# q and k of batches 4 to 7 by GpSimd casts and transfer transposes, global sums and v's copies moved to the period's head

## The chip, the cores and the metric

The kernel runs on one core of one Trainium2 chip. The time is that of one execution on the device, in microseconds (us); before the change it is 334.76 us, the median of 14 runs (332.55 to 339.53). All row times below count from the start of the profiled execution's span.

## What is computed

Two layers in one kernel, for 8 batches of 576 rows: an attention with a window and global rows, then an MLP mixer (over rows, then over channels). Cut to what matters:

```
q, k, v: [8, 8, 576, 64] float32         # batch, head, row, dim
mask = |i - j| <= 32, or i is one of 8 global rows, or j is one
attn = softmax(where(mask, q k^T / 8, -1e9))
x = (attn v), heads side by side         # [8, 576, 512]
h = relu(x^T w_tok1) w_tok2              # over rows: 576 -> 256 -> 576
u = x + h^T
out = u + relu(u w_ch1) w_ch2            # over channels: 512 -> 1536 -> 512
```

Only the window and the global rows and columns are computed; the rest of the scores is never formed.

## The kernel before

**Stages.** Per batch b, all in float16 with float32 sums. `load_qk` and `load_rest` (lines 114 to 120) bring q and k in float32 by SP's DMA queue into `lq`, `lk` (512 rows, four consecutive rows per partition) and `lqr`, `lkr` (the last 64 rows); there is one such buffer of each. `cast_qk` (380) makes float16 copies `qn`, `kn` (two buffers each), for one head pair or, with p None, the last rows. `T` (396) transposes one head pair of q and of k by eight TensorE matmuls with the identity into PSUM, and `TE` (417) copies the result in row order into `qTs`, `kTs` (one DVE copy each, lines 406 and 412). `TR` (421) does the last 64 rows, `globals_` (391) puts the eight global queries into `qTs`. `S_` (443) computes a head pair's windowed scores (22 small matmuls in two parts), `SX` (466) takes the exponential on ScalarE into `e_all`, and `SM` (472) multiplies by the masks on DVE (`eg` at line 476, `e_all` twice at 481). `GK` (508) makes the scores of the global rows, with an exponential into `lf` and a mask product (532). `load_v16` (358) loads v straight to float16 by GpSimd's DMA queue, five transfers, into `vsh`; `v_odd` (371) makes `vod`, a copy of v moved by 64 partitions, by two DVE copies of 64x2112 (373, 374). `OG` (534) sums v over the global rows (20 matmuls) and spreads the result over blocks into `rf` on DVE (544). `PV` (647) makes one 128-row tile of the attention from `lf` x `rf` and `e_all` x `vsh`/`vod`, and normalizes it on DVE (678, 679). `M1` and `M2` (684, 708) are the mixer over rows, with the sum u on DVE (721, 724); `M3` (726) transposes u by DMA transposes on SP's queue. `M4` and `M4l` (749, 760) are the first channel matmul with relu on ScalarE, `M5` (774) the second, in halves of six matmuls of 128x512, with the last sum on DVE (785, 788) into `osb`, which SP writes out. Batches share the last 64 rows in pairs, so `M4l` and a fifth `M5` tile stand in odd periods only.

**Order.** Every engine runs its own instructions in the order in which they are written; the program is written as a weave. "Period b" is the loop's pass b (line 1037): its dense units are `dense(b)` (M4, M4l, M5 of batch b), and between them stand units of the batches behind: in the first half those of n = b + 1 (PV, M1, M2, M3) and the casts and transposes of m = b + 2, in the second half scores and masks of m. `play` (822) walks a list written out by hand, in which each `D` stands for the next dense unit. Period 0 has its own list (`period_0`, 835), and period 1 is woven by cost (`merge` with `sparse2`, 796). Periods 2 to 7 use `first_half` (852) and `second_half` (880); the first half holds the first 12 dense units (15 in odd periods), the second the rest, those left over coming last. "Head b" is the start of the first half of period b.

Before the change the head has M4, M4, then PV; OG and the masks come at the end of the second half before it, and v_odd between the third and the fourth scores. The ten casts of m stand between the units of the first half on ScalarE; three of the four transposes stand late in the first half, the fourth in the second half.

**Buffers.** PSUM is handed out in turn by three pools: `pss` (two buffers of two banks), `psv` (one of two banks) and `psm` (two of one bank). M4 and M5 use `psm`; each tile there waits until the one two before it has been read out. Scores use `pss`; OG, GK, even PV tiles and odd-numbered T use `psv` in most batches.

Of the kernel before, what the change touches and what calls it, by code (L numbers as in the profile page):

```python
# [9 lines left out]
F16 = mybir.dt.float16  # L10
# [5 lines left out]
P = 128  # L16
NT = 5
NG = 8
WIN = 32
GW = 2 * NG  # L20
QS = P + NG
HQ = 64
# [22 lines left out]
def kernel(  # L45
# [12 lines left out]
    nc = tc.nc  # L58
# [312 lines left out]
    def v_odd(b, hs=slice(0, H), eng=nc.vector):  # L371
        i = b % 2
        eng.tensor_copy(out=vod[i][HQ:P, :, hs], in_=vsh[i][HQ:P, 0 : NT - 1, hs])  # L373
        eng.tensor_copy(out=vod[i][0:HQ, :, hs], in_=vsh[i][0:HQ, 1:NT, hs])  # L374

    def castv(p):
        hs = slice(2 * p, 2 * p + 2)
        nc.gpsimd.tensor_copy(out=vsh[0][:, :, hs, 0:D], in_=lv[:, :, hs])
# [9 lines left out]
    def casts(b):  # L388
        return [lambda ti=ti, p=p: cast_qk(b, ti, p, nc.scalar.copy) for p in (None, 0, 1, 2, 3) for ti in range(2)]
# [27 lines left out]
    def TE(b, p):  # L417
        TEq(b, p)
        TEk(b, p)

    def TR(b):
        pr = (psm if b in (0, 2) else psv)([P, 2, 4, NP * 16], name=f"pr_{b}")
        sel = ident.rearrange("p (n r x) -> p r n x", n=NP, r=2)
        for ti, n in enumerate((qr, kr)):
            for i in range(4):
                for par in range(2):
                    nc.tensor.matmul(
                        pr[64 * par : 64 * par + 64, ti, i, :], lhsT=n[b % 2][:, i, :], rhs=sel[:, par], start=True, stop=True
                    )
        st[b]["pr"] = pr  # L430
        if b > 0:
            TRE(b)
# [39 lines left out]
    def SM(b, p):  # L472
        e2 = e_all[:, 2 * p : 2 * p + 2]
        if b > 0:
            gc = bass.AP(tensor=e2.tensor, offset=e2.offset, ap=[e2.ap[0], [QS, NT], [ES, 2], [1, NG]])
            nc.vector.tensor_tensor(
                out=eg[:, :, 2 * p : 2 * p + 2, 0:NG], in0=gc, in1=egm.unsqueeze(2).to_broadcast([P, NT, 2, NG]), op=ALU.mult
            )
        bm = bandm.rearrange("p c x -> p (c x)")[:, 0:ES]
        for par in range(2):  # L480
            nc.vector.tensor_mul(out=e2[:, par], in0=e2[:, par], in1=bm)  # L481
# [26 lines left out]
    def GK(b):  # L508
        s = st[b]
        ps = (psv if b != 2 else pss)([P, 2, 512], name=f"gk_{b}")  # L510
        for p in range(NP):
            o = ps[32 * p : 32 * p + 32]
            qv = qTs[b % 2][:, p, :, NG:QS]
            w = kgz[:, b, p, :]
            nc.tensor.matmul(o[:, 0, 0:384], lhsT=w, rhs=qv[:, 0:3], start=True, stop=True)
            nc.tensor.matmul(o[:, 1, 0:128], lhsT=w, rhs=qv[:, 3], start=True, stop=True)
            nc.tensor.matmul(o[:, 1, 128:192], lhsT=w, rhs=qv[:, 4, 0:LAST], start=True, stop=True)
        s["gk"] = ps
        if b > 0:
            LX(b)  # L520
            LM(b)
# [12 lines left out]
    def OG(b):  # L534
        s = st[b]
        ps = (psv if b != 2 else pss)([P, 2, VW], name=f"og_{b}")
        for c in range(NT):
            for p in range(NP):
                nc.tensor.matmul(
                    ps[32 * p : 32 * p + 32], lhsT=eg[:, c, 2 * p : 2 * p + 2, :],  # L540
                    rhs=vsh[b % 2][:, c, 2 * p : 2 * p + 2, :], start=(c == 0), stop=(c == NT - 1),
                )
        rf = mb.tile([P, NP, 2, VW], F16, tag="rf", name=f"rf_{b}")
        nc.vector.tensor_tensor(
            out=rf, in0=ps.unsqueeze(1).to_broadcast([P, NP, 2, VW]),
            in1=blk.rearrange("p (n r) -> p n r", r=2).unsqueeze(3).to_broadcast([P, NP, 2, VW]), op=ALU.mult,
        )
        s["rf"] = rf
# [243 lines left out]
    def t(b, p):  # L792
        T(b, p)
        TE(b, p)

    def sparse2():
        b, n = 2, 3
        cs = casts(n)

        def cast(k):  # L800
            return [(0.0, c) for c in cs[2 * k : 2 * k + 2]]

        u = [(0.0, lambda: (load_rest(n), load_qk(n, slice(0, H))))]
        u += [(1.0, s2(b, 1)), (0.0, lambda: SM(b, 1)), (1.0, lambda: t(b, 3)), (1.5, s2(b, 2)), (0.0, lambda: SM(b, 2)), (0.0, lambda: v_odd(b))]
        u += [(0.3, lambda: GK(b)), (0.3, lambda: S_(b, 3, 0)), (1.8, lambda: S_(b, 3, 1)), (0.0, lambda: SM(b, 3))]
        u += [(2.5, lambda: OG(b))]
        u += [(2.0, lambda: PV(b, 0)), (2.0, lambda: PV(b, 1)), *cast(0), (2.0, lambda: PV(b, 2)), *cast(1)]
        u += [(0.0, lambda: PV(b, 3)), (1.0, lambda: [M1(b, ch) for ch in range(3)]), *cast(2)]
        u += [(2.0, lambda: PV(b, 4)), *cast(3), (3.0, lambda: [M1(b, ch) for ch in range(3, NT)]), *cast(4)]
        u += [(0.0, lambda: (load_rest(n + 1), load_qk(n + 1, slice(0, H))))]  # L810
        u += [(0.0, lambda: load_v16(n))]
        u += [(1.3, lambda: (M2(b, 0), M3(b, 0))), (1.0, lambda: (M2(b, 1), M3(b, 1)))]
        u += [(2.0, lambda: (M2(b, 2), M3(b, 2) if b % 2 else None))]
        u += [(1.0, lambda: (globals_(n), TR(n)))]
        u += [(1.2, lambda p=p: t(n, p)) for p in range(NP)]
        for p in range(NP):
            u += [(0.3, lambda p=p: S_(n, p, 0)), (2.2, lambda p=p: S_(n, p, 1)), (0.0, lambda p=p: SM(n, p))]
            if p == 2:
                u += [(0.5, lambda: GK(n)), (0.0, lambda: v_odd(n))]
        return u  # L820

    def play(steps, d):
# [9 lines left out]
    def s2(b, p):  # L832
        return lambda: (S_(b, p, 0), S_(b, p, 1))

    def period_0():
        n, m = 1, 2
        D = None
        c2 = casts(m)
        c1 = [lambda ti=ti, p=p: cast_qk(1, ti, p, nc.scalar.copy) for p in (2, 3) for ti in range(2)]
        u = [D, D, D, D, D, D, lambda: TR(n), lambda: globals_(n), D, lambda: t(n, 0), *c1[:2], D]  # L840
        u += [lambda: t(n, 1), *c1[2:], lambda: (load_qk1(2), load_v16(2)), D, s2(n, 0), D, lambda: t(n, 2), lambda: SM(n, 0), D, s2(n, 1), D]
        u += [lambda: t(n, 3), lambda: SM(n, 1), s2(n, 2), lambda: v_odd(n), D, lambda: SM(n, 2), lambda: GK(n), s2(n, 3), D]
        u += [lambda: SM(n, 3), lambda: OG(n), D, lambda: PV(n, 0), lambda: PV(n, 1), D, lambda: PV(n, 2), lambda: PV(n, 3), D]
        u += [*c2, lambda: PV(n, 4), lambda: [M1(n, ch) for ch in range(NT - 1)], D, lambda: M1(n, NT - 1), lambda: globals_(m), D]
        u += [lambda: M2(n, 0), lambda: M2(n, 1), lambda: TR(m), D, lambda: M3p(n, 0), lambda: t(m, 0)]
        u += [lambda: M3p(n, 1), lambda: (M2(n, 2), M3(n, 2)), lambda: t(m, 1)]
        u += [s2(m, 0), lambda: t(m, 2), lambda: SM(m, 0)]
        return u

        return u  # L850

    def first_half(b):
        n, m = b + 1, b + 2
        D = None
        cs = casts(m) if m < B else []

        def c(k):
            return cs[2 * k : 2 * k + 2]

        def tt(p):  # L860
            return [lambda: t(m, p)] if m < B else []

        def pv(tau):
            return lambda: PV(n, tau)

        if n == B:
            return []
        u = [D, *([lambda: OG(n)] if b == 2 else []), D, pv(0), pv(1), *c(0), D, *c(1), D, pv(2), pv(3), *c(2), D, lambda: [M1(n, ch) for ch in range(3)], D]
        if b == 2:
            u += [lambda: gather_t(1)]  # L870
        u += [pv(4), *c(3), D, lambda: M1(n, 3), D, *([lambda: TR(m)] if m < B else []), lambda: M1(n, 4), *c(4)]
        if m < B:
            u += [lambda: load_v16(m), lambda: globals_(m)]
        if m + 1 < B:
            u += [lambda: (load_rest(m + 1), load_qk(m + 1, slice(0, H)))]
        u += [D, *tt(0), D, lambda: (M2(n, 0), M3(n, 0)), D, *tt(1), lambda: (M2(n, 1), M3(n, 1)), D, *tt(2)]
        u += [lambda: (M2(n, 2), M3(n, 2) if n % 2 else None), D]
        return u

    def second_half(b):  # L880
        m = b + 2
        D = None
        if m >= B:
            return []
        return [D, s2(m, 0), D, lambda: t(m, 3), lambda: SM(m, 0), D, s2(m, 1), D, lambda: SM(m, 1), D, s2(m, 2), D,
                lambda: SM(m, 2), lambda: GK(m), lambda: v_odd(m), s2(m, 3), D, lambda: SM(m, 3), D, lambda: OG(m)]

    def dense(b):
        u = [(0.86, lambda j=j: M4(b, j)) for j in range(NJ)]
# [188 lines left out]
```

## Time and profile before

| | |
|---|---|
| median of 14 runs | 334.76 us |
| the profiled execution | 337.63 us, span 335.5 us |
| PE busy | 313.8 us (94% of the span) |
| DVE busy | 192.3 us (57%) |
| ScalarE (ACT) busy | 155.3 us (46%) |
| GpSimd (POOL) busy | 62.6 us (19%) |
| ScalarE casts of q and k, line 386 | 54 of 0.61 to 0.62 us |
| DVE copies of T's results, lines 406 and 412 | 60 of 0.68 us |
| SP's DMA transposes, line 733 | 24, median 1.34 us from one to the next |

How to read it: busy time is the sum of the instructions' durations on an engine. A matmul's duration contains its way through the pipeline (0.38 us for 128x512), while the next starts 0.216 us after it, so the distance of starts, not the duration, says what one costs. In the rows of the trace, "x4" stands for four instructions merged, the first number is the start, the second the duration, and brackets at the end of a row give how long the engine had been idle and who released it. SPq is SP's instruction queue, with the time to issue a transfer, not to move it.

### The profile page before, as it was taken

The numbers are of one execution on the slowest core, as the hardware profiler recorded it, in microseconds if no ns is written. First come the engines' busy times: TensorE is split into PE (matmuls) and PEld (weight loads), VectorE is DVE, ScalarE is ACT, GpSimd is POOL, SyncE is SP. The second block draws the span as 40 slices with busy tenths as digits, with TensorE's granted clock in tenths as the row PEclk, the third lists the DMA queues.
The fourth block names the chain that finished last, engine by engine and source line by source line (L and its number), as shares of the span: only waits on it lengthen the run. The fifth ranks groups of instructions, "written<-read, shape, count | busy, mean of one in ns | idle before, by whom it ended". The sixth has DMA issues, their size and how long they took to land.

```text
span 335.5 us, 8236 instructions
## 1 busy us (share of the span) xinstructions
PE 313.8 (94%) x3505; PEld 173.6 (52%) x3505; DVE 192.3 (57%) x414; ACT 155.3 (46%) x281; POOL 62.6 (19%) x95
## 2 busy tenths in 40 slices
PE   4789989798899999999999999999999999999994
PEld 4557845445456545454456545554556445444641
DVE  7385557859942877486838385377737574331021
ACT  3460378703767055644475435735474333504600
POOL 5795578220031002200130003100000000000000
PEclk9996799999999999999999999999999999999999
DMA  7899998992857944988297716795003121051013
GB/s 214 198 157 228 273 180 234 179 123 48 265 57 68 294 144 69 68 256 138 67 102 225 122 64 106 62 274 150 33 0 59 57 78 33 2 141 63 2 65 91
DMA packets 78198, 41.85 MB, mean 125 GB/s; under 512 B 54482, under 2 KB 72274, under 8 KB 78162
## 3 DMA queue, kind: packets, MB, share of 16 engines
q0 software_dynamic: 38608, 12.88, 31.7%
q1 hardware_dynamic: 39552, 28.45, 31.4%
q8 instruction: 27, 0.44, 0.6%
q14 instruction: 9, 0.07, 0.1%
q10 hardware_dynamic: 2, 0.00, 0.0%
HBM read 36.11 MB, written 9.44 MB: 136 GB/s over the span
## 4 chain that ended last, share of the span: by engine, by line
PE 67%; DVE 12%; DMA 12%; issue 3%; POOL 2%; SPq 2%; ACT 1%; POOLq 0%; DVEq 0%; ACTq 0%
PE op L781 24%; PE b1p L755 19%; DMA wc<-in_moe_w_ch_dram 8%; PE a1p L692 5%; PE hp L716 4%; DMA lq<-in_q_dram 3%; PE pv L656 3%; PE b1lp L768 3%; PE pv L665 3%; PE pT L400 2%; PE s L458 2%; DVE e_all L481 2%; DVE vod L373 1%; DVE vod L374 1%; DVE osb L785 1%
## 5 line engine op out<-in xcount | busy, mean ns | idle before, releaser
L755 PE MATMUL b1p<-uT,wc 128*128 128x512 f16 x384 | 94.9, 380 | 0.8 <-ACT b L758 0.6
L758 ACT ACTIVATE b<-b1p 128x512 f16<-128x512 f32 x96 | 57.0, 598 | 77.0 <-PE b1p L755 76.8
L781 PE MATMUL op<-wc,b 128*128 128x512 f16 x384 | 90.0, 380 | 0.0
L470 ACT ACTIVATE e_all<-s 128x544 f16<-128x544 f32 (+1 forms) x64 | 40.8, 686 | 38.0 <-issue 26.0
L755 PEld LDWEIGHTS <-wc 128*128 128x128 f16 x384 | 34.9, 98 | 39.8 <-issue 2.2
L781 PEld LDWEIGHTS <-b 128*128 128x128 f16 x384 | 35.1, 98 | 39.0
L361 POOL DMA_DIRECT2D vsh<-in_v_dram x35 | 29.4, 845 | 138.5 <-DVE rr L678 124.1
L785 DVE TENSOR_TENSOR osb<-u,op 128x512 f32<-128x512 f16 x32 | 21.9, 686 | 53.1 <-PE op L781 51.0
L679 DVE TENSOR_TENSOR x<-pv,rr 128x512 f16<-128x512 f32 (+1 forms) x35 | 24.2, 691 | 1.2
L481 DVE TENSOR_TENSOR e_all<-e_all,bandm 128x616 f16<-128x616 f16 x56 | 24.3, 475 | 1.0
L678 DVE RECIPROCAL rr<-pv 128x8 f32<-128x8 f32 (+1 forms) x35 | 7.1, 203 | 30.9 <-PE pv L665 30.9
L406 DVE COPY qT<-pT 128x512 f16<-128x512 f16 x30 | 20.5, 685 | 7.2 <-PE pT L400 6.0
L721 DVE TENSOR_TENSOR u<-x,hp 128x1024 f16<-128x1024 f16 x14 | 17.0, 1217 | 12.1 <-PE hp L716 12.1
L412 DVE COPY kT<-pT 128x512 f16<-128x512 f16 x30 | 20.4, 680 | 1.4 <-PE pT L400 0.9
L716 PE MATMUL hp<-a,w 128*128 128x512 f16 x72 | 19.1, 379 | 1.3 <-DVE u L721 1.3
L656 PE MATMUL pv<-rf,lf 128*64 128x264 f16 x126 | 18.3, 283 | 0.9 <-DVE kgz L355 0.7
L458 PE MATMUL s<-qT,kT 64*64 64x136 f16 (+2 forms) x704 | 16.2, 215 | 2.1 <-ACT kT L412 1.0
L386 ACT CAST qn<-lq 128x512 f16<-128x512 f32 x27 | 16.6, 613 | 3.3 <-DMA lq<-in_q_dram 3.3
L665 PE MATMUL pv<-vsh,e_all 128*64 128x66 f16 x280 | 18.0, 194 | 0.0
L665 PEld LDWEIGHTS <-e_all 128*64 128x64 f16 x504 | 17.9, 111 | 0.0
L458 PEld LDWEIGHTS <-kT 64*64 64x64 f16 x704 | 10.7, 107 | 13.4 <-issue 10.7
L386 ACT CAST kn<-lk 128x512 f16<-128x512 f32 x27 | 16.8, 621 | 0.9 <-DMA lk<-in_k_dram 0.9
(175 smaller groups left out, 362.7 us busy)
## 6 DMA issues: line engine op xcount, KB each, us to landing
out_dram<-osb SPq DMA_DIRECT2D x32, 256.0 KB
lq<-in_q_dram SPq DMA_DIRECT2D x5, 1024.0 KB
lk<-in_k_dram SPq DMA_DIRECT2D x5, 1024.0 KB
wc<-in_moe_w_ch_dram POOLq DMA_DIRECT2D x6, 512.0 KB
vsh<-in_v_dram POOLq DMA_DIRECT2D x21, 128.0 KB
lq<-in_q_dram POOLq DMA_DIRECT2D x2, 1024.0 KB
lk<-in_k_dram POOLq DMA_DIRECT2D x2, 1024.0 KB
vsh<-in_v_dram POOLq DMA_DIRECT2D x14, 96.0 KB
```

Source lines behind the costliest of these rows:

```text
L361: nc.gpsimd.dma_start(out=vsh[b % 2][r0:r1, c, :, 0:D], in_=v[b, :, j0 : j0 + (r1 - r0), :].rearrange("h p d -> p h d"),)
L386: eng(out=(qn, kn)[ti][b % 2][:, :, hs].rearrange("p i h d -> p h i d"), in_=(lq, lk)[ti][:, hs])
L458: nc.tensor.matmul(ps[o, par, i0 - a : i1 - a], lhsT=kT[r, HQ * j : HQ * j + HQ], rhs=qf[r, i0:i1], start=b > 0, stop=b > 0 or j in js[-2:],)
L470: nc.scalar.activation(out=e2[:, :, a:z], in_=ps[:, :, 0 : z - a], func=AF.Exp, scale=scale)
L481: nc.vector.tensor_mul(out=e2[:, par], in0=e2[:, par], in1=bm)
L656: nc.tensor.matmul(ps[r0 : r0 + 64, hf, 0 : NP * VW], lhsT=s["lf"][:, HQ * t : HQ * t + HQ], rhs=s["rf"][:, 2 * hf : 2 * hf + 2], start=Tr ...
L665: nc.tensor.matmul(ps[r0 : r0 + 64, hf, VW * hh : VW * hh + VW], lhsT=e_all[:, h, lo : lo + HQ], rhs=(vod if t % 2 else vsh)[b % 2][:, tau ...
L716: nc.tensor.matmul(ps[:, i, :], lhsT=w2[:, ch, P * tau - sh : P * tau - sh + P], rhs=s["a1"][:, ch, :], start=(ch == 0), stop=(ch == 1),)
L755: nc.tensor.matmul(ps, lhsT=wc1[:, cc, P * j : P * j + P], rhs=s["uT"][:, cc, :], start=(cc == 0), stop=(cc == 3))
L758: nc.scalar.activation(out=s["b1"][:, j, :], in_=ps, func=AF.Relu)
L781: nc.tensor.matmul(ps, lhsT=w, rhs=wc2[:, j, :], start=(j == 0), stop=(j == NJ - 1))
L785: nc.vector.tensor_add(out=osb, in0=s["u16"][:, tau], in1=ps)
```

## The change

q and k of batches 4 to 7 are cast on GpSimd (`casts_g`, written at the head of the period), transposed from SBUF to SBUF by eight DMA transposes on SP's queue (`QT`, into new buffers `qraw` and `kraw`, of which there is one each), and put into row order by four GpSimd copies for q (`TSq`, first half) and four ScalarE copies for k (`TSk`, start of the second half). For those batches the casts on ScalarE, the 32 TensorE transposes and the eight DVE copies per batch are gone. `load_v16(m)` stands behind `TSq`. OG of batch n, for n from 3 on, stands after the first dense unit of the period's head, and `v_odd` just before it (both before: in the second half of the period before, OG of batch 3 excepted). The v copy of batch 1 is made by two DMAs on SP's queue, and the results of `TR(1)` use `pss`. The second half's list is spaced anew.

```
+    def v_odd_dma(b):
+        i = b % 2
+        nc.sync.dma_start(out=vod[i][HQ:P], in_=vsh[i][HQ:P, 0 : NT - 1])
+        nc.sync.dma_start(out=vod[i][0:HQ], in_=vsh[i][0:HQ, 1:NT])
...
+    qraw, kraw = [const.tile([P, NP, 4, P], F16, name=f"{n}raw") for n in "qk"]
+
+    def QT(b):
+        for ti in range(2):
+            for i in range(4):
+                nc.sync.dma_start_transpose(
+                    out=(qraw, kraw)[ti][:, :, i, :], in_=(qn, kn)[ti][b % 2][:, i].rearrange("p h d -> p (h d)")
+                )
+
+    def TSq(b):
+        for p in range(NP):
+            nc.gpsimd.tensor_copy(
+                out=qTs[b % 2][:, p, 0:4, NG:QS].rearrange("p t (x i) -> p t x i", i=4),
+                in_=qraw[:, p].rearrange("p i (t x) -> p t x i", t=4),
+            )
+
+    def TSk(b, p):
+        nc.scalar.copy(
+            out=kTs[b % 2][:, p, WIN : WIN + 512].rearrange("p (x i) -> p x i", i=4),
+            in_=kraw[:, p].rearrange("p i x -> p x i"),
+        )
+
+    def casts_g(b):
+        for ti in range(2):
+            for p in (None, 0, 1, 2, 3):
+                cast_qk(b, ti, p, nc.gpsimd.tensor_copy)
+
     def TR(b):
-        pr = (psm if b in (0, 2) else psv)([P, 2, 4, NP * 16], name=f"pr_{b}")
+        pr = (psm if b in (0, 2) else pss if b == 1 else psv)([P, 2, 4, NP * 16], name=f"pr_{b}")
...
@@ sparse2 (period 1) @@
             if p == 2:
-                u += [(0.5, lambda: GK(n)), (0.0, lambda: v_odd(n))]
+                u += [(0.5, lambda: GK(n))]
...
@@ period_0 @@
-        u += [lambda: t(n, 3), lambda: SM(n, 1), s2(n, 2), lambda: v_odd(n), D, lambda: SM(n, 2), lambda: GK(n), s2(n, 3), D]
+        u += [lambda: t(n, 3), lambda: SM(n, 1), s2(n, 2), lambda: v_odd_dma(n), D, lambda: SM(n, 2), lambda: GK(n), s2(n, 3), D]
...
@@ first_half @@
-        u = [D, *([lambda: OG(n)] if b == 2 else []), D, pv(0), pv(1), *c(0), D, *c(1), D, pv(2), pv(3), *c(2), D, lambda: [M1(n, ch) for ch in range(3)], D]
+        u = [lambda: casts_g(m)] if m < B else []
+        u += [D, lambda: v_odd(n), lambda: OG(n), D, pv(0), pv(1), D]
+        if m < B:
+            u += [lambda: QT(m), lambda: TSq(m), lambda: load_v16(m)]
+        u += [D, pv(2), pv(3), D, lambda: [M1(n, ch) for ch in range(3)], D]
         if b == 2:
             u += [lambda: gather_t(1)]
-        u += [pv(4), *c(3), D, lambda: M1(n, 3), D, *([lambda: TR(m)] if m < B else []), lambda: M1(n, 4), *c(4)]
+        u += [pv(4), D, lambda: M1(n, 3), D, *([lambda: TR(m)] if m < B else []), lambda: M1(n, 4)]
         if m < B:
-            u += [lambda: load_v16(m), lambda: globals_(m)]
+            u += [lambda: globals_(m)]
         if m + 1 < B:
             u += [lambda: (load_rest(m + 1), load_qk(m + 1, slice(0, H)))]
-        u += [D, *tt(0), D, lambda: (M2(n, 0), M3(n, 0)), D, *tt(1), lambda: (M2(n, 1), M3(n, 1)), D, *tt(2)]
+        u += [D, D, lambda: (M2(n, 0), M3(n, 0)), D, lambda: (M2(n, 1), M3(n, 1)), D]
         u += [lambda: (M2(n, 2), M3(n, 2) if n % 2 else None), D]
...
@@ second_half @@
-        return [D, s2(m, 0), D, lambda: t(m, 3), lambda: SM(m, 0), D, s2(m, 1), D, lambda: SM(m, 1), D, s2(m, 2), D,
-                lambda: SM(m, 2), lambda: GK(m), lambda: v_odd(m), s2(m, 3), D, lambda: SM(m, 3), D, lambda: OG(m)]
+        return [D, lambda: [TSk(m, p) for p in range(NP)], s2(m, 0), D, D, lambda: SM(m, 0), s2(m, 1), D, D, lambda: SM(m, 1),
+                s2(m, 2), D, lambda: SM(m, 2), lambda: GK(m), D, s2(m, 3), lambda: SM(m, 3), D]
```

More of the change, by code (lines that the diff above doesn't have):

```diff
@@ L854, in first_half @@
         D = None
[L855 to L861, printed above, removed]
         def pv(tau):
```

## The prediction

> **What bounds the kernel now.** I read the page's 40 slices first, then the time-ordered rows of PE, DVE, GpSimd and SP over one even and one odd period, and last the waits. Slices:
>
> ```profile
> PE   4789989798899999999999999999999999999994
> DVE  7385557859942877486838385377737574331021
> ACT  3460378703767055644475435735474333504600
> POOL 5795578220031002200130003100000000000000
> ```
>
> From slice 14 on (118 us) PE is at 9, and nothing else is. A PE row's length contains pipeline latency, so I count starts: from the first M4 matmul of batch 3 (162.89) to that of batch 5 (236.66) are 73.8 us. The pair's work counted at start-to-start pace (128x512: 0.216 us, 128x128: 0.0556 us, S_ 0.40 per head pair, a PV tile 0.97) is about 73: PE has almost no holes in periods 2 to 5. The rows of period 3 that the change touches:
>
> ```profile
> 176.62 0.39 PE L400 MATMUL pT<-ident,qn 128*128 128x128 f16 x4
> 176.84 0.39 PE L400 MATMUL pT<-ident,kn 128*128 128x128 f16 x4
> 177.06 1.03 PE L755 MATMUL b1p<-uT,wc 128*128 128x512 f16 x4
> ...
> 182.77 0.59 PE L716 MATMUL hp<-a,w 128*128 128x512 f16 x2 [0.33 <-DVE u L721]
> ```
>
> Eight transposes (one head pair) hold PE for 177.06 - 176.62 = 0.44 us; a period has four such sets. The 0.33 us hole is M2's third part waiting for DVE, which has four TE copies between the M2 sums; each of periods 2 to 5 has it. The head of period 3, PE then DVE:
>
> ```profile
> 159.06 0.46 PE L458 MATMUL s<-qT,kT 64*64 64x72 f16 x22
> 159.46 2.76 PE L781 MATMUL op<-wc,b 128*128 128x512 f16 x12
> 162.15 0.80 PE L539 MATMUL og<-vsh,eg 128*32 128x132 f16 x20
> 162.89 2.13 PE L755 MATMUL b1p<-uT,wc 128*128 128x512 f16 x8
> 164.95 0.30 PE L656 MATMUL pv<-rf,lf 128*64 128x264 f16 x2
> ```
>
> ```profile
> 160.89 0.71 DVE L373 COPY vod<-vsh 64x2112 f16<-64x2112 f16 x1
> 161.63 0.70 DVE L374 COPY vod<-vsh 64x2112 f16<-64x2112 f16 x1
> 162.26 0.18 DVE L476 TENSOR_TENSOR eg<-e_all,egm 128x80 f16<-128x80 f16 x1
> 162.47 0.87 DVE L481 TENSOR_TENSOR e_all<-e_all,bandm 128x616 f16<-128x616 f16 x2
> 163.26 0.68 DVE L785 TENSOR_TENSOR osb<-u,op 128x512 f32<-128x512 f16 x1
> 163.86 0.70 DVE L544 TENSOR_TENSOR rf<-og,blk 128x528 f16<-128x528 f32 x1
> ```
>
> Here DVE runs back to back: v_odd, the last mask products, osb, rf. PV needs rf. From the last scores to PV are 5.89 us against 0.40 + 12 x 0.216 + 0.74 + 8 x 0.216 = 5.46 of work: a hole of 0.4. One wait of period 0, and two rows for new costs:
>
> ```profile
> 61.59 0.46 PE L539 MATMUL og<-vsh,eg 128*32 128x132 f16 x17 [1.75 <-DVE eg L476]
> ```
>
> ```profile
> 180.24 5.97 SPq L733 DMA_TRANSPOSE uT<-u  x4
> ```
>
> ```profile
> 20.75 0.72 POOL L378 CAST vsh<-lv 128x640 f16<-128x640 f32 x1 [0.17 <-DMA lv<-in_v_dram]
> ...
> 21.00 0.77 DVE L373 COPY vod<-vsh 64x528 f16<-64x528 f16 x1
> ...
> 22.40 0.29 DVE L373 COPY vod<-vsh 64x528 f16<-64x528 f16 x1
> ```
>
> **What the Trainium skill says.** SBUF — State Buffer, section SBUF: two separate sides: DVE and GpSimd share a port pair under an exclusive lock held for a whole instruction; a DVE copy in a two-port mode, or a DVE operation with two SBUF inputs, blocks against GpSimd. The trace agrees for the copy: at 21.00 it waits until the GpSimd cast is over (21.47) and takes 0.77 us, alone 0.29. It shows no case with two SBUF inputs (L481 is 0.47 to 0.48 in all 56). GPSIMD Engine Reference, section 3.1: 769 ns for 512 elements of a tight one-input loop; here 640 elements took 0.72 to 0.77 us, and the two 512-element casts, beside DVE casts, 1.02 and 0.80. VectorE: DVE Perf Modes, section The three transpose paths: 1309 ns for a 128x128 transpose by DMA; here SP needs a median 1.34 us to issue one of 128x512, four such blocks.
>
> **The change, part by part.**
>
> (1) PE transposes of batches 4 to 7 go, with TE: 4 periods x 4 sets x 0.44 = 7.0 us of PE time in full periods. DVE loses 8 copies of 0.6 us per period, so M2's sums follow at once, and the 0.33 us hole goes four times: 1.3. Together -8.3.
>
> (2) The casts leave ACT (8 x 0.5 plus 2 x 0.3 us of its time per period) for GpSimd, whose queue is idle there (a 31 us wait at the longest). They hang on nothing but the landing of q and k, issued about 14.6 us into the period before and landed about 10 us later. So, although written at the head, they run in the second half before it: 2 x (0.35 + 4 x 0.6 to 0.9) = 6 to 8 us. PE does not wait for them.
>
> (3) QT: eight transposes on SP, 8 x 1.34 = 10.7 us of issue, from about head + 2 (behind the last output) to + 12.7, landed by + 13.7. Behind them in SP's queue stand the q and k loads (now about + 13 to + 15, before at + 14.6) and M3's transposes (needed at about + 15, for the next period): neither loses much. TSq on GpSimd starts at about + 8.5, four strided copies not shown by the trace, between 0.6 us each (the cast) and three times that: done by + 11 to + 16. load_v16 queues behind it on GpSimd, a few us later than now, for data used at the next head. The first scores come at head + 20.2 in an even period (224.03 - 202.49 = 21.5, less 3 x 0.44 and 0.33, plus 0.3), + 23.7 in an odd one. TSk: four ACT copies of 0.59 us (ACT's copy of this shape from PSUM), right behind the last relu; the first ends before the 1.3 us of M5 that stand ahead of the scores do. All hidden: 0.
>
> (4) The head. v_odd now stands between osb and rf, and one of two M5 halves that covered the last mask products comes earlier. Even period before it (heads 3, 5), from the start of the last scores: exp ends + 1.75 (before + 2.03, at 161.09, with GK's two small exponentials ahead of it, which are now done by then), mask products 1.0, osb 0.6, v_odd 1.37, rf 0.7: + 5.4, PV at + 5.5. PE has 0.40 + 1.30 + 0.74 + 1.73 = 4.2 of work. Hole 1.3 against 0.4: + 0.9 each. Odd (heads 4, 6): the fifth tile's osb ends + 5.0, v_odd, rf: + 7.1 against 6.8 of work, before 0.25 of hole: + 0.2 each. Head 2: osb has to wait for its matmuls (126.4) where v_odd filled that time: rf 130.2 for 129.7, + 0.5. Sum + 2.7.
>
> (5) Period 0. v's copy leaves DVE for two SP transfers; SP has nothing else from the input loads until 61.46, so they run when v is in, some 15 us before use: 1.45 us off DVE ahead of eg. But osb (its matmuls end at 59.4) and the exp (59.8) then come last: OG resumes at about 60.45 for 61.59, -1.2. TR(1) in another PSUM buffer: T(1,0) no longer waits 0.35 for its evacuation, -0.4. Together -1.6.
>
> (6) The port. Casts in a second half meet mask products; one that is blocked costs PE nothing while DVE has slack (about 7 us of work in 14), but at a head DVE is the chain. Ends: 0, and a cast of 0.6 us ahead of each of the five two-port operations there (eg, two e_all, two copies) at heads 2 to 5: 4 x 3.0 = 12. The casts should end around head - 3 of the next, so I take + 0.4 per head, + 1.6.
>
> Sum: -8.3 + 2.7 - 1.6 + 1.6 = **-5.6 us**. The profiled execution took 337.63 (span 335.5 and 2.1 around it), which gives 332.0. It lies 2.87 above the median of the runs; the sum is made of PE pace and waits, so I take it off the median too: 334.76 - 5.6 = 329.2.
>
> **Rivals.** *Nothing is lost at the heads*: if v_odd runs in a gap and no cast collides, -8.3 - 1.6 = -9.9, 324.9. For: DVE is down by 5 us a period. Against: the row order above. *Half of the port's upper end*, 6.5 us: -0.7, 334.1. *Slower, the port*: q and k land late enough (after about head + 25, with 8 us of casts) that casts still run under the last mask products and v_odd; it cancels the gain at 1.8 us per head, and at the full 12 us gives -7.2 + 12 = +4.8, 339.6. For: the copy of 0.77 us above. Against: the landing about 10 us after issue. *Slower, the transposes*: TSk should start at head + 20.2 - 1.3 = 18.9 in even periods; with a start at + 2 and 1 us to land, above (18.9 - 3) / 8 = 2.0 us each k's land too late. The median is 1.34, the longest single one 2.9, the worst four 7.39 us beside the q and k loads; at 2.9 even periods lose 7.5 and odd ones 4: 23 in all, about 352.
>
> **Numbers.** Forecast 0.50, nothing lost 0.17, half the port 0.10 (0.04 of it faster, 0.06 same), the port 0.17 (0.01 same), transposes 0.06. A measurement of this kernel tells about 0.3% (1 us) from no change. Faster 0.71, same 0.07, slower 0.22. The range, 324.5 to 337.0, takes in the full gain and the lower part of the port case, and leaves out the late transposes and the rest of the port.
>
> **What would show it.** The 73.8 us between batches 3 and 5 should become about 71.5. No hole on hp (L716); PV at the even heads waiting for rf; OG of batch 1 waiting under 0.7 us. Casts on GpSimd ending before each head, L373 at 0.71 there; scores (L458) waiting for no copy. L481 far above 0.48, or v_odd over 1 us, speaks for the port; PE idle ahead of L458 for the transposes; PE pace off 0.216 us would upset all of it.

## The result and the profile after

The changed kernel takes 338.99 us (median of 10 runs, 337.78 to 341.21; one further run took 335.87); beside it on the same chip the kernel before took 335.01. The ratio is **1.0138 [1.0115, 1.016]**: 4.6 us slower, where 5.6 faster was forecast. Its profiled execution took 341.76 us (span 340.0). In 8 of the 13 profiled executions the granted TensorE clock is at half for some microseconds somewhere ahead of the end, at places that differ (28 to 38 us in the profile of before, 63 to 70 in that of after), so I compare periods 2 to 5 in the traces, where it is full except in runs 3 and 6, and take the rest from ratios of runs.

The slices of after, PE and GpSimd:

```profile
PE   4788998598899998999699899999799899999994
POOL 5695469120000230456036500636063000000000
```

PE was at 9 from slice 14 on; now it falls to 6 and 7 at the heads of periods 3 and 5, and to 5 (from 7) at 60 us. PE's busy time went from 313.8 to 305.2 us, yet the span grew by 4.4. The places, first the middle of period 3 (PE's timeline; the bracket is PE's idle time and who ended it):

```profile
184.34 1.03 PE L748 MATMUL hp<-a,w 128*128 128x512 f16 x4
185.21 1.03 PE L787 MATMUL b1p<-uT,wc 128*128 128x512 f16 x4
186.07 0.59 PE L748 MATMUL hp<-a,w 128*128 128x512 f16 x2
...
191.01 0.46 PE L490 MATMUL s<-qT,kT 64*64 64x72 f16 x22 [0.37 <-ACT kT L443]
191.40 2.76 PE L813 MATMUL op<-wc,b 128*128 128x512 f16 x12
194.47 0.31 PE L490 MATMUL s<-qT,kT 64*64 64x72 f16 x10 [0.30 <-ACT e_all L502]
195.10 0.35 PE L490 MATMUL s<-qT,kT 64*64 64x72 f16 x12 [0.32 <-ACT e_all L502]
```

The transposes are gone and the third part of M2 (hp, x2) no longer waits. But the scores now wait three times, 1.0 us together: first for a k copy, then for the exponential that frees their PSUM buffer. ACT at the same place shows why:

```profile
189.38 0.60 ACT L804 ACTIVATE b1l<-b1lp 128x512 f16<-128x512 f32 x1 [0.30 <-PE b1lp L800]
189.88 4.02 ACT L443 COPY kT<-kraw 128x512 f16<-128x512 f16 x4
193.78 2.52 ACT L502 ACTIVATE e_all<-s 128x544 f16<-128x544 f32 x4
```

Four k copies take 4.0 us, not 4 x 0.59, and the first exponentials stand behind all of them. The price of 0.59 was that of this row of before, a ScalarE copy in the same order into the same tile, but out of PSUM:

```profile
9.71 0.59 ACT L412 COPY kT<-pT 128x512 f16<-128x512 f16 x1
```

Now the head of period 3, PE and then DVE:

```profile
163.33 1.47 PE L813 MATMUL op<-wc,b 128*128 128x512 f16 x6
166.43 1.02 PE L787 MATMUL b1p<-uT,wc 128*128 128x512 f16 x4 [1.63 <-DMA uT<-u]
167.39 0.47 PE L571 MATMUL og<-vsh,eg 128*32 128x132 f16 x20
168.00 1.02 PE L787 MATMUL b1p<-uT,wc 128*128 128x512 f16 x4
170.08 0.30 PE L688 MATMUL pv<-rf,lf 128*64 128x264 f16 x2 [1.06 <-DVE rf L576]
```

```profile
167.25 0.69 DVE L817 TENSOR_TENSOR osb<-u,op 128x512 f32<-128x512 f16 x1 [1.50 <-DMA out_dram<-osb]
167.97 0.71 DVE L373 COPY vod<-vsh 64x2112 f16<-64x2112 f16 x1
168.71 0.70 DVE L374 COPY vod<-vsh 64x2112 f16<-64x2112 f16 x1
169.34 0.69 DVE L576 TENSOR_TENSOR rf<-og,blk 128x528 f16<-128x528 f32 x1
```

Two waits: M4 for the transposed u, and PV for rf, which stands behind osb and v_odd as the prediction's step (4) had it. DVE's osb, in turn, had waited 1.50 us for an output to leave. The wait for u comes from SP's queue (start, time to issue):

```profile
131.81 5.59 SPq L431 DMA_TRANSPOSE qraw<-qn  x4
137.49 6.24 SPq L431 DMA_TRANSPOSE kraw<-kn  x4
...
149.34 9.76 SPq L765 DMA_TRANSPOSE uT<-u  x4
159.19 2.11 SPq L768 DMA_TRANSPOSE uTl<-ul  x1
161.40 6.90 SPq L818 DMA_DIRECT2D out_dram<-osb  x4
```

M3's four transposes take 9.76 us (5.97 in the row shown of before), and the outputs stand behind them. Last, batch 1 in period 0:

```profile
58.23 0.46 PE L571 MATMUL og<-vsh,eg 128*32 128x132 f16 x17 [0.72 <-DVE eg L508]
...
63.99 0.26 PE L697 MATMUL pv<-vod,e_all 128*64 128x66 f16 x1 [3.65 <-DMA vod<-vsh]
```

OG waits 0.72 us for 1.75, about as forecast, but PV then waits 3.65 for the copied v. SP issued the two transfers, 264 KB each, as soon as v was in, at 53.0 and 53.7; the loads of q, k and v of batch 2 were issued from 52.0 to 59.5 on GpSimd's queue, and the copy was there 11 us later. PE's windows after it (PE busy with its instructions in brackets, granted clock, DMA share, GB/s):

```profile
62.00:64.00 2.00, 0.01 (x2) 0.81 0.99 273
64.00:66.00 2.00, 2.00 (x38) 0.50 1.10 373
66.00:68.00 2.00, 2.00 (x6) 0.50 2.35 163
68.00:70.00 2.00, 2.00 (x37) 0.50 2.55 153
```

The clock falls to half at about 63 us, still in that idle time, and stays there for six microseconds after it; six matmuls of M5 took 2.74 us there for 1.47.

The balance, from the first M4 of one batch to that of another:

| stretch | before | after | kernel of run 9 below |
|---|---|---|---|
| batch 2 to batch 6 (periods 2 to 5) | 149.90 | 150.08 | 141.61 |
| batch 6 to the end of the span | 59.3 | 60.3 | 59.3 |
| batch 0 to batch 1 (period 0) | 42.74 | 48.88 | 43.91 |

So periods 2 to 5 neither gained nor lost, head 6 lost 1.0, and period 0 lost 6.1, of which 2 to 3 us are the clock of this one execution (an estimate: run 7 below, with a full clock, takes 46.71 there, and half of six microseconds is 3).

### The profile page after: what moved, and what is told of

Same layout as the page of the kernel before. It is cut to its first block, busy times and chain, and to the rows that moved or that the text cites. A ratio compares the mean times of both kernels' runs of the same rounds, so it can differ in the third digit from the quotient of the medians.

```text
span 340.0 us, 8075 instructions
## 1 busy us (share of the span) xinstructions
PE 305.2 (90%) x3377; PEld 164.1 (48%) x3377; DVE 176.8 (52%) x380; ACT 153.8 (45%) x257; POOL 100.6 (30%) x151
## 5 line engine op out<-in xcount | busy, mean ns | idle before, releaser
L813 PE MATMUL op<-wc,b 128*128 128x512 f16 x384 | 91.3, 384 | 0.0
L437 POOL COPY qT<-qraw 128x512 f16<-128x512 f16 x16 | 16.3, 1061 | 64.6 <-DMA qraw<-qn 64.6
L513 DVE TENSOR_TENSOR e_all<-e_all,bandm 128x616 f16<-128x616 f16 x56 | 26.3, 510 | 1.0
L688 PE MATMUL pv<-rf,lf 128*64 128x264 f16 x126 | 19.5, 297 | 5.8 <-DVE rf L576 5.0
L490 PE MATMUL s<-qT,kT 64*64 64x136 f16 (+2 forms) x704 | 17.2, 216 | 6.1 <-ACT e_all L502 3.1
L697 PEld LDWEIGHTS <-e_all 128*64 128x64 f16 x504 | 19.3, 117 | 4.0 <-DMA vod<-vsh 3.8
L697 PE MATMUL pv<-vsh,e_all 128*64 128x66 f16 x280 | 19.5, 200 | 0.0
L697 PE MATMUL pv<-vod,e_all 128*64 128x66 f16 x224 | 15.6, 202 | 3.6 <-DMA vod<-vsh 3.6
L391 POOL CAST qn<-lq 128x512 f16<-128x512 f32 x17 | 10.0, 633 | 27.8 <-DMA lq<-in_q_dram 27.8
L688 PEld LDWEIGHTS <-lf 128*64 128x64 f16 x126 | 9.2, 114 | 15.7 <-issue 11.1
```

Source lines behind the costliest of these rows:

```text
L490: nc.tensor.matmul(ps[o, par, i0 - a : i1 - a], lhsT=kT[r, HQ * j : HQ * j + HQ], rhs=qf[r, i0:i1], start=b > 0, stop=b > 0 or j in js[-2:],)
L688: nc.tensor.matmul(ps[r0 : r0 + 64, hf, 0 : NP * VW], lhsT=s["lf"][:, HQ * t : HQ * t + HQ], rhs=s["rf"][:, 2 * hf : 2 * hf + 2], start=Tr ...
L697: nc.tensor.matmul(ps[r0 : r0 + 64, hf, VW * hh : VW * hh + VW], lhsT=e_all[:, h, lo : lo + HQ], rhs=(vod if t % 2 else vsh)[b % 2][:, tau ...
L813: nc.tensor.matmul(ps, lhsT=w, rhs=wc2[:, j, :], start=(j == 0), stop=(j == NJ - 1))
```

## The experiments

Two theories stood at the start. **A**: v's copy by transfers costs period 0 several microseconds, and the gain of periods 2 to 5 is spent on waits which the new order makes. **B**, its rival: that copy is not what makes the kernel slower. "Ratio" is always that to the kernel before on the same chip.

**1. v's copy of batch 1 back on DVE.**

```
-        ... s2(n, 2), lambda: v_odd_dma(n), D, ...
+        ... s2(n, 2), lambda: v_odd(n), D, ...
```

> The changed kernel with one part undone: batch 1's copy of v is made by DVE again (v_odd), not by two transfers. Theory A (the copy by transfers costs period 0 its wait: PV of batch 1 stands 3.65 us for vod, and that is most of the 4.6 us by which the change is slower): 4 to 5 us less than the changed kernel, that is 334 to 335.5, within 1 us of the kernel before; periods 2 to 6 unchanged. Rival B (that wait only takes the place of a later one in period 0, since q and k of batch 2 land late as well; the loss is made at the period heads): within 1 us of the changed kernel, 338 to 340.

Measured: 1.0016 [0.9969, 1.0064], about 4 us under the changed kernel; PV waits for no transfer, and OG waits 1.43 us. The heads still wait for rf (1.56, 1.06, 0.63, 1.07, 0.63 us) and one of them for u (0.77). Batch 2 to 6 takes 148.47 for 150.08 with the same instructions; the difference is the wait for u, 0.77 for 2.36. A stands for period 0; it did not foresee that the wait for u would change.

**2. The kernel before with that copy by transfers, and nothing else.**

> The kernel before with that one part of the change alone: batch 1's copy of v by two transfers on SP's queue. Theory A: 3.5 to 6 us slower than the kernel before (338.5 to 341), with PV of batch 1 waiting 3 us or more for vod. Rival B: within 1 us of the kernel before.

Measured: 1.0055 [1.0024, 1.0086], +1.8 us. PV waits 2.56 us and OG 0.72 for 1.75; the clock stays at 1.00 behind it. The mechanism is there without the rest of the change; the size is under what A said (3.5 to 6 us, a wait of 3 or more).

**3. Run 1 with OG, v_odd and the second half's spacing as before the change.**

```
-        u += [D, lambda: v_odd(n), lambda: OG(n), D, pv(0), pv(1), D]
+        u += [D, *([lambda: OG(n)] if b == 2 else []), D, pv(0), pv(1), D]
...
+                lambda: SM(m, 2), lambda: GK(m), lambda: v_odd(m), s2(m, 3), D, lambda: SM(m, 3), D, lambda: OG(m)]
```

> As the first run (batch 1's v copy on DVE), and OG and v_odd back in the second half, with the units of the second half spaced as before; casts on GpSimd, transposes by transfer and the copies TSq and TSk stay. Theory A (the heads hold back about 1 us each, five of them, since v_odd now stands on DVE between the last masks and rf): 3 to 5 us less than the first run, about 330 to 332, below the kernel before. Rival C (what is gained at the heads is lost again, since u's transposes or the scores come late there, so that the wait only changes its name): within 1 us of the first run.

Measured: 1.0193 [1.0118, 1.0269], 6 us *slower* than run 1. The waits for rf are gone, but OG of batches 3 and 5 waits 2.73 and 4.35 us. In this trace the clock is also at 0.50 for about 3.3 us behind the first of these waits and 7 us around the second, so that not all of the loss is waiting: batch 2 to 6 takes 155.40 us, 6.9 more than in run 1, and I estimate 4 of them for the clock (half of the 8 us in which PE worked at half clock). DVE ahead of the second of these:

```profile
235.10 0.71 DVE L373 COPY vod<-vsh 64x2112 f16<-64x2112 f16 x1 [3.37 <-DMA vsh<-in_v_dram]
236.28 0.70 DVE L374 COPY vod<-vsh 64x2112 f16<-64x2112 f16 x1 [0.48 <-DMA vsh<-in_v_dram]
```

v_odd stands in the second half again, but v isn't there: `load_v16` now stands behind `TSq` on GpSimd, which waits for the transposes. DVE holds the mask products behind v_odd. Both expectations fell, and run 5 tests what this suggests: that v_odd can't stand earlier without waiting, as long as v's loads are so late.

**4. Run 1 with v's loads ahead of the transposes.**

```
-            u += [lambda: QT(m), lambda: TSq(m), lambda: load_v16(m)]
+            u += [lambda: load_v16(m), lambda: QT(m), lambda: TSq(m)]
```

> As the first run, and load_v16(m) stands ahead of QT and TSq on GpSimd's queue, so that v's transfers start at the head and do not meet q's, k's and u's. Theory A (u's transposes took 9 to 10 us for four because v, q and k are loaded beside them; M4 of the next batch waits 1.6 and 0.7 us for them at the even heads): 1.5 to 2.5 us less than the first run, and no wait of M4 for uT. Rival D (the transposes are slow because of SP's own queue, eight more of them and the outputs, whatever is loaded): within 1 us of the first run, the wait for uT stays.

Measured: 0.9988 [0.994, 1.0035], which can't be told from run 1. No M4 waits for u now (nor in the traces of 5, 6, 9 and 11, which all have this edit); batch 2 to 6 takes 147.70. The waits for rf and of the scores are unchanged. M3's transposes in period 2:

```profile
142.77 5.34 SPq L765 DMA_TRANSPOSE uT<-u  x4
```

In periods 2 to 4 they take 5.34, 6.24 and 7.49 us, against 8.63, 11.35 and 10.42 in run 1, so v's loads beside them do slow them, as A said. The time that A forecast was not gained, for run 1 had only 0.77 us of this wait left. Nor are v's loads all of it: in run 5, with v's loads out of their way too, they take 7.2 to 8.2 us.

**5. Both: v's loads first, heads as before.**

> OG, v_odd and the spacing of the mask products back in the second half, as in the run with the old heads, but now with v's loads issued ahead of the transposes and of TSq. Theory (the old heads lost 6 us only because v landed late: DVE stood at v_odd, waiting for v's load, 2.4 us in period 2 and 3.9 us in period 4, with the mask products, osb and rf queued behind it): v_odd waits for nothing now, the waits for rf at heads 3 to 6 (0.6 to 1.1 us) are gone, and the time is 2 to 4 us under that of v's loads first with the new heads: a ratio to before of 0.985 to 0.993. Rival (DVE is short of time in the second half whatever v does): the OG of batches 3 and 5 still waits over 1.5 us for eg, ratio over 1.005.

Measured: **0.9873 [0.9839, 0.9908]**. No PV of batches 3 to 7 waits for rf; batch 2 to 6 takes 145.62, 2.1 less than in run 4, and batch 6 to the end 59.3 for 60.4. So the heads cost 3.2 us, and what had forced them was the place of v's loads (run 3 with them late, this run with them early). What is left in periods 2 to 5 are mostly the scores' waits: those of 0.28 us and more come to 3.2 us.

**6. Run 5 with each k copy just ahead of its scores.**

```
-        return [D, lambda: [TSk(m, p) for p in range(NP)], s2(m, 0), D, ...
+        return [D, k_(0), s2(m, 0), D, lambda: SM(m, 0), D, k_(1), s2(m, 1), ... lambda: v_odd(m), k_(3), s2(m, 3), ...
```

> The kernel of the run before, with each k copy (TSk) just ahead of the scores that use it, not all four ahead of the first. Theory (four copies of 0.98 us stand ahead of the first exponential on ACT, so scores wait for a free PSUM buffer, 0.3 to 0.35 us two or three times a period): these waits fall by half or more and the time drops by another 1 to 3 us, ratio 0.98 to 0.99. Rival (the wait is for PSUM, which two score tiles fill whatever ACT does first; or a k copy now stands directly ahead of its scores): within 1 us of the run before, or slower by as many k-copy waits as it has sets, 0.3 each.

Measured: 0.9977 [0.9948, 1.0007], 1% slower than run 5. Most of the short waits went, and a long one came: the fourth scores of batches 4 to 7 wait 1.81 or 1.82 us each for their k. ACT:

```profile
228.23 1.26 ACT L502 ACTIVATE e_all<-s 128x544 f16<-128x544 f32 x2 [0.85 <-ACT kT L443]
230.13 0.49 ACT L559 ACTIVATE lf<-gk 128x384 f16<-128x384 f32 x1 [0.65 <-PE gk L549]
230.52 0.33 ACT L560 ACTIVATE lf<-gk 128x192 f16<-128x192 f32 x1
230.73 1.08 ACT L443 COPY kT<-kraw 128x512 f16<-128x512 f16 x1
```

The copy stands behind the exponentials of GK, which wait for PE, and PE waits for the copy. The rival was right in kind, though each wait is six times the 0.3 us that it named: four copies in one block cost less than a copy that sits on the way to its own scores. Behind the first of these waits the clock is at 0.50 for about 3.5 us as well (158 to 161.5 us), behind the other three it is not.

**7. The changed kernel with 40 spare matmuls in the wait for v's copy.**

```
-        u += [lambda: SM(n, 3), lambda: OG(n), D, lambda: PV(n, 0), ...
+        u += [lambda: SM(n, 3), lambda: OG(n), D, lambda: W(40, True), lambda: PV(n, 0), ...
```

> The changed kernel with 40 matmuls of 128x128 that write a spare PSUM tile, ahead of batch 1's first PV, in the wait for v's copy: 40 x 0.056 = 2.2 us of work in a wait of 3.65 us. Nothing else is changed. Theory (the wait was long enough for the granted clock to fall to 0.50 for some 6 us after it, which costs 2.7 us beside the wait): the wait left is about 1.4 us, the clock stays at 1.00 from 63 to 70 us, and the time falls 2 to 2.7 us below the changed kernel's, a ratio to before of 1.004 to 1.009. Rival (the clock fell for another reason, or fell in that one execution only): the ratio stays at 1.011 to 1.016.

Measured: 1.014 [1.0099, 1.0182]. The clock stayed at 1.00, but PV started at 64.28 (63.99 before the filling), since the transfers set its time, and no time was gained in the runs. The transfers landed no earlier, so that a wait of 3.01 us was left where 1.4 was expected. The half clock was seen in one execution of the changed kernel; that its other runs lose by it is not shown.

**8. The changed kernel with v's transfers on GpSimd's queue, ahead of batch 2's loads.**

```
-        ... lambda: (load_qk1(2), load_v16(2)), D, ...
+        ... lambda: (v_odd_dma(n), load_qk1(2), load_v16(2)), D, ...
```

> The changed kernel with v's two transfers of batch 1 on GpSimd's queue, right ahead of the loads of q, k and v of batch 2, instead of on SP's beside them. They still wait for v, so the loads of batch 2 start about 1 us later. Theory (the transfers took 11 us because they share the DMA engines with 2.3 MB of loads that were issued about when they were): they land by about 58 us, no PV waits for them, the clock stays at 1.00, and the ratio is that of the copy left on DVE, 0.997 to 1.005. Rival (copying 528 KB from SBUF to SBUF is itself that slow): the PV still waits over 2 us and the ratio stays above 1.008.

Measured: 1.0046 [1.0011, 1.0081], 3 us under the changed kernel. No PV waits for v. In the profiled execution (338.82 us, among the longest of its runs) PE waits elsewhere, PE first and then ACT:

```profile
72.95 3.87 PE L748 MATMUL hp<-a,w 128*128 128x512 f16 x8 [3.55 <-ACT a L729]
```

```profile
68.67 0.62 ACT L391 CAST kn<-lk 128x512 f16<-128x512 f32 x1 [2.69 <-DMA lk<-in_k_dram]
...
72.32 0.59 ACT L729 ACTIVATE a<-a1p 128x512 f16<-128x512 f32 x1
```

Batch 2's k lands late: its first cast starts at 68.67, as in the changed kernel (67.99) and later than in run 1 without the transfers (63.52). The casts on ACT stand ahead of a relu that PE needs, and PE waits there; the clock is at 0.50 from 72 to 78.5 us. So copying 528 KB is not slow in itself (PV reads it from 59.0 us on): beside the loads it is late, and with it the loads are late, in either order.

**9. Run 5 with three of the four k copies in the first half.**

```
-        u += [D, D, lambda: (M2(n, 0), M3(n, 0)), D, lambda: (M2(n, 1), M3(n, 1)), D]
+        u += [D, D, lambda: (M2(n, 0), M3(n, 0)), *k_(0), D, lambda: (M2(n, 1), M3(n, 1)), *k_(1), D]
...
-        return [D, lambda: [TSk(m, p) for p in range(NP)], s2(m, 0), D, ...
+        return [D, lambda: TSk(m, 3), s2(m, 0), D, ...
```

> The kernel of v's loads first with the old heads (ratio 0.9873), with three of the four k copies in the first half, one behind each part of M2, where ACT has gaps of 1.1 us between relus; the fourth stays ahead of the first scores. Theory (the scores' waits of 0.28 to 0.35 us, 3.8 us in periods 2 to 5 together, come from four copies of 1 us that stand ahead of the first exponential on ACT): the waits fall to under 1 us in all, and the time is 2 to 3.5 us below: ratio 0.977 to 0.982. Rival (k is not there yet, so a copy holds relus behind it and PE waits for b1p or b instead): within 1 us of that kernel or slower, with PE waits for kraw, b1p or b of 0.3 us and more.

Measured: **0.9728 [0.9657, 0.9799]** (median 326.56 of 6 runs), 9 us under the kernel before. The profiled execution, 331.09 us, is the longest of the six; the clock is full in its periods 2 to 6 (it is at half at 28 to 38.5 and 62.5 to 65.5 us). Its second half in period 3 on PE, and the k copies in period 4 on ACT:

```profile
185.66 0.46 PE L490 MATMUL s<-qT,kT 64*64 64x72 f16 x22
186.06 2.76 PE L813 MATMUL op<-wc,b 128*128 128x512 f16 x12
188.75 0.46 PE L490 MATMUL s<-qT,kT 64*64 64x72 f16 x22
189.14 2.76 PE L813 MATMUL op<-wc,b 128*128 128x512 f16 x12
191.84 0.46 PE L490 MATMUL s<-qT,kT 64*64 64x72 f16 x22
```

```profile
215.57 1.07 ACT L443 COPY kT<-kraw 128x512 f16<-128x512 f16 x1
216.80 0.60 ACT L790 ACTIVATE b<-b1p 128x512 f16<-128x512 f32 x1 [0.16 <-PE b1p L787]
217.29 1.06 ACT L443 COPY kT<-kraw 128x512 f16<-128x512 f16 x1
```

A copy of 1.07 us fits the gap between two relus, and no score waits. Batch 2 to 6 takes 141.61 us, 4.0 less than in run 5, and the ratios differ by 4.9 us, more than the 2 to 3.5 that I expected. M3's transposes are as slow as in run 5 (8.44 us for four in period 4, 8.18 there), and nobody waits for them.

**10. The kernel before with its casts on GpSimd, and nothing else.**

```
+        u = [*([lambda: casts_g(m)] if m < B else []), D, ...
```

> The kernel before with the casts of batches 4 to 7 on GpSimd at each period's head, and nothing else: PE's transposes, the heads and v's loads as before. Theory (casts were never on the path and the port costs next to nothing): ratio 0.997 to 1.003, so that all the gain of the best kernel comes from the transposes. Rival (DVE operations that wait for the port behind the casts delay the heads, or v's loads, behind the casts on GpSimd, come late): ratio over 1.004, with waits for eg or rf at the heads over 0.7 us.

Measured: 1.0012 [0.9978, 1.0046]; the mask products take 470 to 481 ns in its trace, and the 0.33 us waits of hp are there as before. The casts cost and bring nothing by themselves.

**11. Run 9 with v's copy of batch 1 by transfers again.**

> The best kernel so far (ratio 0.9728) with one thing put back as the change has it: v's copy of batch 1 by two SP transfers. All else of periods 1 to 6 stays. It tells what that one part costs, which two pairs of runs gave differently: +4.1 us (the changed kernel, 1.0138, against the same with the copy on DVE, 1.0016) and +1.8 us (the kernel before with and without it). Theory A (the wait for the transfers and the late casts behind it cost what the trace shows: 3.65 us at PV less 0.7 at OG, and more where the granted clock falls): +3 to +4.5 us, ratio 0.982 to 0.987, PV of batch 1 waiting 2.5 us and more. Rival (the true size is that of the kernel before with the transfers): +1.8 us, ratio about 0.978, PV waiting under 2 us.

Measured: 0.9778 [0.9701, 0.9855], 1.7 us over run 9, and the intervals overlap, so it doesn't tell the two sizes apart. The ratio is the rival's, the trace is A's: PV waits 3.37 us for vod, and batch 0 to 1 takes 46.99 us for 43.91 (in both traces with some 3.5 us at half clock).

## Why the prediction was wrong, step by step

**(1) PE's transposes and the hole on hp, -8.3: right; that it is right to a tenth is luck.** From batch 2 to 6 run 9 takes 149.90 - 141.61 = 8.29 us less than before. Counted from start to start, the 16 sets of transposes of before take 7.8 us there (0.49 each, where I had 0.44 from one of them), and the four holes 1.3; two waits of run 9 that before does not have, 0.47 and 0.35 us of OG for eg, take 0.8 back. The gain was all there; the change spent it again in the same periods.

**(2) Casts hidden: right** (run 10).

**(3) "All hidden: 0": wrong, the largest miss.** Two terms failed. *The k copies*: I priced them at 0.59 us each, from ACT's copy of this shape and order out of PSUM. Out of SBUF it takes 1.05 to 1.10 us, and four stand 4.0 us ahead of the exponentials. I looked only at when the first ends, though the later scores need the exponentials behind the fourth. Cost over periods 2 to 5: 145.62 - 141.61 = 4.0 us (run 5 against 9). *M3's transposes*, "neither loses much": they took 8.75 to 10.44 us for 5.8 to 6.8, and M4 of two batches waited 1.63 and 0.73 us for them. This wait differs between executions (0.77 in run 1, 3.25 in run 7, 0.47 in run 8, each for one batch), and it is gone in every trace with v's loads first: 2.4 us in the changed kernel's profile (150.08 - 147.70). I had also passed `load_v16` "a few us later" as harmless; runs 3 and 5 show that this is what ties v_odd to the head.

**(4) The heads, +2.7: right in mechanism, somewhat small.** Measured 3.2 (run 4 against 5: 2.1 in periods 2 to 5 and 1.1 behind). The waits for rf are 1.06 where I had holes of 1.3 (heads 3 and 5), 0.63 where I had 0.45 (heads 4 and 6), and 1.56 at head 2, where before its OG waited 0.69.

**(5) Period 0, -1.6: wrong in sign.** "They run when v is in, some 15 us before use": v was in at 53.0, 7 us before PV could start, and the transfers took 11 us beside the loads of q and k, 2.3 MB, and those of v. I had looked at SP's queue, which was free, and not at the DMA engines, which were busy all the time (share 0.99 to 1.07 from 56 to 64 us). The saving ahead of OG was there (1.0 us), PV's wait ate it about three times over. Net cost in traces without a fall of the clock: 45.23 - 42.74 = 2.5 us (run 2) and 46.71 - 43.19 = 3.5 (run 7 against 1); in runs 1.7 (run 11) and 1.8 (run 2) to 4.1 (run 1). What it is exactly stays open; I take about 3.

**(6) The port, +1.6: not there at the heads.** The mask products (L513) have a median of 478 ns for 476; the longest is 879, and none over 0.5 us lies less than 6 us before a head. What the Trainium skill says in SBUF — State Buffer, section SBUF: two separate sides, is borne out where casts run beside them (two took 1.57 us for 0.87 in run 3, at 149.19), but that falls in the second half, where DVE has time. The sign "v_odd over 1 us" did come, in run 9: while GpSimd issued v's loads, a copy of v_odd took 1.08 us (0.71 before), and OG behind it waited for eg.

```profile
156.99 4.21 POOL L361 DMA_DIRECT2D vsh<-in_v_dram  x5
```

```profile
160.65 1.08 DVE L373 COPY vod<-vsh 64x2112 f16<-64x2112 f16 x1
```

```profile
162.62 0.46 PE L571 MATMUL og<-vsh,eg 128*32 128x132 f16 x17 [0.47 <-DVE eg L508]
```

It did so again at 231.07 (0.95 us, OG waiting 0.35). Over all traces, from period 1 on, a copy of v_odd that no issue of v's loads overlaps took 0.70 to 0.71 us; 15 are overlapped (runs 5, 6, 9 and 11), and 11 of these took 0.85 to 1.18. That fits the port; no run moves these loads alone, so it isn't shown by experiment.

The sum with what was measured: -8.3 + 4.0 + 2.4 + 3.2 + 3.0 = +4.3 us, against 4.6. In periods 2 to 5 it must close, since each term is the step from one trace to the next. The ratios of runs, each uncertain by one to three microseconds, give for the same five terms -9.1, +4.9, +0.9, +3.9 and +4.1: the wait for u is the one that they don't tell from nothing. My rival "slower, the port" named 339.6 us, close to the result, but for a cause that isn't there in the changed kernel; "slower, the transposes" had the right queue with far too large a price, at the wrong end (PE didn't wait for k's transposes but for u's behind them). Of what I said would show it, the missing hole on hp, rf at the heads, OG's wait (0.72 for "under 0.7") and L373 at 0.71 came as described; "scores waiting for no copy" and the 71.5 us between batches 3 and 5 (73.58 measured: 240.01 - 166.43) did not.

## What to carry to other kernels

This is what one kernel showed. Taking work off the bounding engine is worth its full time only if nothing that replaces it stands in an in-order queue ahead of something that engine needs soon: count the whole block of moved instructions up to the last one, on each queue, and ask what stands behind it. A slow replacement is harmless in a gap of its queue (run 9) and costly directly ahead of its user, in one block (run 5) or one at a time (run 6). A transfer that replaces a copy on an engine has to be priced by what else the DMA engines carry at that time, not by whether the issuing queue is free.

## What the hardware did that I had not expected

A ScalarE copy of 128x512 float16 that reads SBUF with a stride took 1.05 to 1.10 us, against 0.59 for the same copy, with the same stride, out of PSUM; ScalarE's casts of 128x512, which read SBUF without a stride, took 0.61. So neither the stride nor SBUF alone made it slow; why both together do was not tested. The strided GpSimd copies for q took 1.05 to 1.07. SP needed 5.79 us to issue the four 128x512 DMA transposes of period 2 before, and 9.76 close behind the issue of v's loads. The Trainium skill, in TensorE: Matmul & The Clock Gate, section 🎯 Why this matters for your kernels, warns of idle gaps of over about 3 us between matmuls. Here the clock fell to 0.50 behind or in idle times of 4.35 (run 3), 3.65 (the changed kernel), 3.55 (run 8) and 3.37 us (run 11), but also behind 2.73 (run 3), 1.81 (run 6, one of four such) and 1.75 (runs 5, 6 and 9), and not behind 3.01 (run 7), 2.56 (run 2) or the 1.75 of the kernel before. So in these traces the length of a single gap doesn't decide it, and what does stays open.
